# Blockwise-causal attention into a ReGLU layer on one core: two heads normalised in one piece, and new hand-listed orders for tiles 3 to 8

## The chip, the core and the metric

The kernel runs on one core of a Trainium2 chip. Its engines work side by side, each through its own instruction list, and wait for each other by semaphores: TensorE (PE) multiplies matrices into PSUM banks, VectorE (DVE), ScalarE (ACT) and GpSimd (POOL) work on elements, and SyncE (SP) issues transfers; ACT and POOL issue some as well. The metric is device microseconds of one execution, as the median of several runs.

## The reference

Eight batches of eight heads attend to themselves over 576 positions of 64 numbers, each block of 64 positions seeing its own and the earlier blocks. The heads are laid side by side to 4608 rows of 512, which go through a gated layer.

```python
scores = scale * np.matmul(q, k.transpose(0, 1, 3, 2))      # q, k, v: (8, 8, 576, 64)
mask = block_i >= block_j                                   # blocks of 64 positions
attn = np.exp(scores - max); attn = attn / (attn.sum(-1) + 1e-09)
x = np.matmul(attn, v).transpose(0, 2, 1, 3).reshape(4608, 512)
out = (np.maximum(x @ w_gate, 0.0) * (x @ w_val)) @ w_out   # 512 -> 1536 -> 512
```

## The kernel before

**Tiles.** The layer works on nine tiles of 512 rows: tiles 0 to 7 are the first 512 rows of each batch, and tile 8 is the 64 last rows of all eight batches together. While PE works on the layer of tile j, the attention of batch j + 1 (in the code `up`) is mixed into the same lists, and the loads and transposes of batch j + 2. From tile 3 on, pairs of output features are computed with seven products of half size in place of eight (`times`, `pair` and `seven_products`), so that DVE, ACT and POOL have adds and copies to do around them.

**Order.** Nothing decides the order at run time. Tiles 3 to 6 run one list of tokens, `ORDER_3_6`, tile 7 runs `ORDER_7` and tile 8 `ORDER_8`; `program(j)` turns each token into instructions, and each engine does its own in the listed order. The tokens that the text speaks of are these:

- `A2`: the scores of round 2 of a batch (a round is a pair of heads), L631, into two tiles of kind sc (two PSUM banks each) and two single banks; `E2t`, `E2u`, `E2f`, `E2s`: its exponentials on ACT (L636, L643); `C20`: zeros in a corner of the weights, a memset on DVE (L1516) or POOL (L1519).
- `V10`: head 0 of round 1 times v on PE (`head_av`, L779 and L793); a column of ones in v gives the sum of the weights as column 64. `N10`: that head is normalised on DVE (`normalise`: reciprocal L716, product into `xnat` L718, product of the last 64 rows into `xtail` L725).
- `T1`: `xnat` of round 1 is transposed into `xT` by a transfer on SP (L862); `T3` also transposes `xtail` (L765). `d0` and `d1` transpose q and k of the batch after (L519), `d2` and `d3` their tails (L524, L526); `l` and `w` load q, k and v by POOL's queue (L509).
- `g`, `v`, `r`, `h`: the plain products with the gate and value weights (L1339), relu, and their product (L1435). `X`, `Y`: sums of x that the seven products need (L1171), `U`: sums of weights (L979).
- `p54`: product 4 of pair 5 (L1363; each such token is two matmuls 128x256, and there are two of each). `p5a`, `p5u`, `p5w`: copies on ACT (L1385); `p5d`, `p5e`, `p5c`: adds on DVE (L1389); `p5r`: relu; `p5H`: product of the upper half with the relu (L1401, DVE or POOL); `p5L`: the lower half's relu and product in one DVE instruction (L1405).
- `s1002`: a part sum for the output products (quad 1, part 0, L1020, DVE or POOL). `M1`: two matmuls of output product 1 (L1061), six times `M1` making the product up; the third and sixth read pairs 4 and 5. `oa`, `ou`, `ow`, `oy`: copies on ACT (L1106; in tile 8 the last one in halves `oya` on ACT and `oyb` on DVE, L1118); `oc`, `od`, `oe`: adds on DVE (L1100), in tile 8 `oca` and `ocb` in halves. `S0`, `S1`, `S2`, `Sa`, `Sya` and so on: stores of the output (L906).

**Banks.** PSUM holds two sc tiles of two banks, one bank `one` and three banks `ffnp`. `AV_BANK` says into which kind `V` writes for each of the four rounds, `PAIR_BANK` and `OUT_BANK` the same for the seven products, and `SLOTS` which buffer each allocation of a kind takes. `ON_POOL` names the tokens that POOL does; the others of the kind are DVE's.

For round 1 the table gives each head an sc tile of its own, of which one bank is used, and `N10` and `N11` follow their heads separately. `normalise_two` and the branch `"sc2"` of `head_av` are in the code already, and no table uses them.

Of the kernel before, what the change touches and what calls it, by code (L numbers as in the profile page):

```python
# [17 lines left out]
def kernel(  # L18
# [24 lines left out]
    OBS = 5  # L43
    SLOTS = {
        "sc": (
            "010101010101010010101010101010101010101010101010101010101001100011000101"
            "1001100011000101100110001100010110011000110001011001011001000"
        ),
        "ffnp": (
            "021021021020210210210210210210120210120202010101210120201201120120210211"  # L50
            "201021102101020120120120121201202101202101202101210201201202120101212012"
            "021021020102121010210201201202120101212012021021020102121010210202102010"
            "2020201210"
        ),
        "ob": (
            "043210432104314021340123401321034120134021034013204103214013210341201340"
            "210340134013204230214302"
        ),
        "gate_sb": (
            "021021021021021021021021021021021021021201201210210212012012102102120120"  # L60
            "1201"
        ),
    }
# [23 lines left out]
        p17*2 p16*2 C00 C01 p1c k V00 N00 P v1*2 p1u p15*2 p1w p1d p14 V01 N01 p14 p1e
        p1L v1*2 r0 r1 p13*2 p1r v0*2 h1 A1 E1t v0*2 h0 p21*2 E1s p22*2 w1 p27*2 p2a
        p26*2 E1u l1 w2 p31 p1H l2 l3 p2c p31 g8 U05 l4 p2w p24*2 w3 s0002 p2u p2e p2L
        l5 l6 p25 g8 p25 p2d C11 p3a p36*2 p32 p37*2 E1f C10 V11 l7 N11 U06 l8 p3u p35  # L90
        p3w p35 p3d g8*2 r8 p23*2 p2H l9 p34*2 p3e p33*2 p3r p32 A2 E2t E2u p3c p3L v8*4
# [9 lines left out]
        p0u p05*2 p21 p0w p1u p21 p04*2 p0d p0e p2a p15*2 p1w p1d p22 p03 p22 p03 p0r
        p31 p14*2 p13*2 p1r p26 p31 p0L p27 p26 p27 p2c p1e p1H Y5 p1L p37*2 p0H s0002
        s0202 s0102 p32*2 p2u p25 p3a p3c p36 p25 p36 p2w p24*2 p2d p2e p51*2 p3w p3u
        p35*2 p3d p23*2 p2L p34*2 p5a p56 p33*2 p2r p2H p3e p3L p52 p57 p56 p41 p57 p41
# [7 lines left out]
        p04 p05*2 p0d p21 p1u p15*2 p31 p1w p1d p14*2 p1e p3a p04 p1L p0e p21 p2a p03*2
        p0r p0H p13 p02 p13 p1r p02 p0c P p1H p36 p26*2 p2u p27*2 p2w p41 p32 p25 p32
        p41 p4a p25 s0002 p0L s0102 p2d p3c p37*2 p3w p36 p3u p24*2 p2e p23*2 p2r p2H
        p34*2 p3e p35 p47 p35 p3d p22*2 p47 p2c p4w p3L p2L p42 p51*2 p5a p42 p33*2 p3r
        p3H p4c p46*2 p56 p44*2 p4u p4e p4L p56 p5u p57*2 p5w p45*2 p4d p55*2 p5d p54*2
# [38 lines left out]
        (6, 5): ('ffn', 'one', 'ffn'),
        (7, 0): ('ffn', 'one', 'one'),
        (7, 1): ('sc', 'sc', 'sc'),
        (7, 2): ('ffn', 'ffn', 'ffn'),
        (7, 3): ('one', 'ffn', 'sc'),
        (7, 4): ('ffn', 'one', 'ffn'),  # L160
        (7, 5): ('sc', 'sc', 'ffn'),
        (8, 0): ('one', 'sc', 'ffn'),
# [6 lines left out]
    ON_POOL = set(
        """  # L170
        33H 35H 3C00 3C01 3C10 3C11 3C20 3C21 3C30 3C31 3X4 3X6 3X7 3s0102
        3s0202 3s0302 3s1302 3s2202 3s2302 43H 45H 4C00 4C01 4C10 4C11 4C20 4C21
        4C30 4C31 4X4 4X6 4X7 4s0102 4s0202 4s0302 4s1302 4s2202 4s2302 53H 55H
        5C00 5C01 5C10 5C11 5C20 5C21 5C30 5C31 5X4 5X6 5X7 5s0102 5s0202 5s0302
        5s1302 5s2202 5s2302 63H 65H 6C00 6C01 6C10 6C11 6C20 6C21 6C30 6C31 6X4
        6X6 6X7 6s0102 6s0202 6s0302 6s1302 6s2202 6s2302 70H 72H 7X4 7X5 7X6
        7Y5 7Y7 7s0102 7s0202 7s0302 7s1002 7s1102 7s1202 7s1302 7s2302 80H 82H
        83H 8s0002 8s0102 8s1002 8s1202 U03 U06 U07 U46
        """.split()
    )  # L180
# [1636 lines left out]
```

## Time and profile before

| what | value |
|---|---|
| median of 3 runs | 344.85 us (344.63 to 344.87) |
| profiled execution, device time | 344.71 us |
| its span, first to last instruction | 342.8 us |
| granted TensorE clock, mean | 0.997 |

The profiled execution is one of its own, beside the three. The profile gives each engine's busy time in the span, the chain of work that ended last, the groups of instructions by line with their mean time, and, on request, the timeline of one engine: start, duration, engine, line, operation, what is written and read, and in brackets how long the engine had been idle and what it waited for. `x15` at the end of a timeline row means that fifteen instructions of one form in a row are shown as one. A queue name with q (`SPq`, `ACTq`) is an engine issuing transfers.

### The profile page before, as it was taken

The page shows a single profiled execution, that of the slowest core. Times are in us where ns is not written, and L with a number is a line of the kernel's source. Part 1 is how long each engine was busy: PE and PEld are TensorE (multiplying, and loading weights), DVE is VectorE, ACT ScalarE, POOL GpSimd, SP SyncE. Part 2 cuts the span into 40 slices and gives each one's busy share as a digit, 9 for nine tenths or more (in the row PEclk, how much of TensorE's full clock was granted, in tenths as well). Part 3 has the DMA queues.
Part 4 walks back from the last instruction along what each step waited for, and adds up shares of the span by engine and source line. Part 5 has one row for each costly group of instructions (what it writes and reads, how often), then busy time and mean ns, then how long its engine had stood idle before and what let it go on. Part 6 is the DMA issues. An engine that isn't in the chain of part 4 may idle for free.

```text
span 342.8 us, 8917 instructions
## 1 busy us (share of the span) xinstructions
PE 332.7 (97%) x3477; PEld 233.8 (68%) x3518; DVE 233.1 (68%) x540; ACT 210.8 (61%) x344; POOL 216.7 (63%) x272
## 2 busy tenths in 40 slices
PE   8899999999999999999999999999999999999994
PEld 4544455545545558777877787777777788888883
DVE  4854445668637887389538972898279958966992
ACT  4942757588325882778558764876488727637731
POOL 2766566488695912787778967986514694750631
PEclk9999999999999999999999999999999999999998
DMA  8999999999998999799899989996510140002004
GB/s 242 294 351 371 368 230 238 240 163 155 187 197 137 144 158 137 165 143 121 111 165 120 130 116 153 128 137 118 138 33 2 33 122 12 2 31 94 33 0 122
DMA packets 155337, 50.06 MB, mean 146 GB/s; under 512 B 134496, under 2 KB 151648, under 8 KB 155296
## 3 DMA queue, kind: packets, MB, share of 16 engines
q0 software_dynamic: 70576, 9.12, 43.6%
q1 hardware_dynamic: 77536, 32.52, 43.0%
q10 hardware_dynamic: 7184, 7.87, 7.8%
q8 instruction: 27, 0.44, 0.5%
q14 instruction: 14, 0.11, 0.1%
HBM read 37.75 MB, written 9.44 MB: 138 GB/s over the span
## 4 chain that ended last, share of the span: by engine, by line
PE 88%; issue 4%; DVE 2%; ACT 2%; POOL 2%; POOLq 0%; DVEq 0%; ACTq 0%
PE ffnp L1179 16%; PE ffnp L1363 9%; PE ffnp L1339 8%; PE sc L1363 8%; PE sc L1061 6%; PE ffnp L1282 6%; PE ffnp L1061 6%; PE one L1363 5%; PE one L1061 4%; PE sc L631 3%; PE one L631 2%; PE one L779 2%; PE ffnp L779 2%; PE one L1179 2%; PE sc L779 1%
## 5 line engine op out<-in xcount | busy, mean ns | idle before, releaser
L636 ACT ACTIVATE attnT<-sc 128x1024 bf16<-128x1024 f32 x56 | 56.7, 1036 | 0.0
L1189 ACT ACTIVATE gate_sb<-ffnp 128x512 bf16<-128x512 f32 x35 | 20.6, 599 | 27.3 <-PE ffnp L1179 24.4
L1179 PE MATMUL ffnp<-xT,wg 128*128 128x512 bf16 x130 | 36.2, 379 | 0.6
L1061 PEld LDWEIGHTS <-stage 128*128 128x128 bf16 x336 | 32.0, 98 | 4.1 <-issue 0.2
L1363 PEld LDWEIGHTS <-stage 128*128 128x128 bf16 x288 | 27.3, 98 | 7.8
L779 PEld LDWEIGHTS <-attnT 128*128 128x128 bf16 x640 | 26.3, 98 | 7.7 <-DVE xnat L718 1.2
L1179 PE MATMUL ffnp<-xT,wv 128*128 128x512 bf16 x108 | 31.3, 380 | 0.2
L1199 DVE TENSOR_TENSOR hT<-gate_sb,ffnp 128x512 bf16<-128x512 bf16 x28 | 19.2, 684 | 14.9 <-PE ffnp L1179 12.0
L1389 DVE TENSOR_TENSOR ob<-ffnp,ob 128x512 f32<-128x512 f32 x29 | 19.8, 684 | 12.6 <-ACT ob L1385 12.6
L509 POOL DMA_DIRECT2D v_bf<-in_v_dram x30 | 24.3, 829 | 6.0 <-PE sc L793 3.1
L1061 PEld LDWEIGHTS <-hT 128*128 128x128 bf16 x252 | 24.2, 98 | 5.3 <-DVE hT L1405 1.1
L1363 PEld LDWEIGHTS <-wg 128*128 128x128 bf16 x224 | 21.9, 98 | 5.1
L1363 PEld LDWEIGHTS <-wv 128*128 128x128 bf16 x224 | 21.5, 98 | 5.3 <-ACT attnT L636 1.1
L1106 ACT COPY ob<-sc 128x512 f32<-128x512 f32 x13 | 7.6, 586 | 28.4 <-PE sc L1061 27.0
L1519 POOL MEMSET attnT<- 64x256 bf16 x34 | 10.2, 314 | 23.4 <-ACT attnT L636 16.0
L1282 PE MATMUL ffnp<-wo,hT 128*128 128x512 bf16 x91 | 23.1, 379 | 0.2
L1179 PEld LDWEIGHTS <-wg 128*128 128x128 bf16 x144 | 13.3, 98 | 13.8 <-issue 0.5
L1179 PEld LDWEIGHTS <-wv 128*128 128x128 bf16 x144 | 13.0, 98 | 14.3 <-issue 1.5
L1334 ACT ACTIVATE gate_sb<-ffnp 128x512 bf16<-128x512 f32 x30 | 17.6, 603 | 8.1 <-PE ffnp L1363 4.6
L509 POOL DMA_DIRECT2D q_bf<-in_q_dram x20 | 18.0, 908 | 5.0 <-DVE recip L752 4.0
L643 ACT ACTIVATE attnT<-one 128x512 bf16<-128x512 f32 (+1 forms) x28 | 15.0, 537 | 9.8 <-PE ffnp L631 8.4
L1020 POOL TENSOR_TENSOR stage<-hT,stage 128x512 bf16<-128x512 bf16 x15 | 17.4, 1167 | 4.2 <-DVE stage L1020 3.6
(228 smaller groups left out, 918.3 us busy)
## 6 DMA issues: line engine op xcount, KB each, us to landing
out_dram<-ob ACTq DMA_DIRECT2D x28, 256.0 KB, 3.4
stage<-in_moe_w_val_dram SPq DMA_DIRECT2D x6, 512.0 KB, 8.7
stage<-in_moe_w_gate_dram SPq DMA_DIRECT2D x6, 512.0 KB, 8.2
stage<-in_moe_w_out_dram SPq DMA_DIRECT2D x6, 512.0 KB, 10.5
q_bf<-in_q_dram POOLq DMA_DIRECT2D x20, 128.0 KB, 4.7
k_bf<-in_k_dram POOLq DMA_DIRECT2D x20, 128.0 KB, 5.5
v_bf<-in_v_dram POOLq DMA_DIRECT2D x20, 128.0 KB, 5.7
stage<-in_v_dram SPq DMA_DIRECT2D x19, 128.0 KB, 5.6
```

The lines of the kernel that those rows point to most:

```text
L509: ins = nc.gpsimd.dma_start(dst, part_of)
L636: return lambda: nc.scalar.activation(at[:, :, lo : lo + 512], sc, AF.Exp, scale=scale)
L779: nc.tensor.matmul(av[:, p, :], at[:, col : col + 128], v_bf[b % 2][:, c, h, :], start=(p == 0), stop=(c == p), skip_group_check=True,)
L1061: nc.tensor.matmul(to, sums.of(c)[which][:, 128 * p : 128 * p + 128], right, start=first, stop=(c == 5), skip_group_check=True,)
L1179: nc.tensor.matmul(to, (wg, wv)[t][f // 4][:, c, 128 * (f % 4) : 128 * (f % 4) + 128], x[:, c], start=(c == 0), stop=(c == 3),)
L1189: nc.scalar.activation(gate_sb, gate, AF.Relu)
L1199: nc.vector.tensor_tensor(out=h, in0=gate_sb, in1=val, op=AX.mult)
L1282: nc.tensor.matmul(op, hT[f][:, 128 * s : 128 * (s + 1)], wo[f // 4][:, f % 4, n0:n1], start=(f == 0), stop=(f == 11),)
L1334: nc.scalar.activation(st[key], of, AF.Relu)
L1339: nc.tensor.matmul(to, (wg, wv)[t][f // 4][:, c, 128 * (f % 4) : 128 * (f % 4) + 128], x[:, c], start=(c == 0), stop=(c == 3),)
L1363: nc.tensor.matmul(st[key][:, 256 * k : 256 * k + 256], left[:, c, 128 * k : 128 * k + 128], right[:, c], start=new and (k, c) == (0, 0), ...
L1389: nc.vector.tensor_tensor(out=t, in0=st[n, of], in1=t, op=AX.add)
```

## The change

In tiles 3 to 6 the two heads of round 1 now write the two banks of one sc tile, one after the other, and one `N11` normalises both: a reciprocal of 128x10, a product of 128x512 into `xnat` and a product of 64x128 into `xtail`. `N10` is gone from the list, and `V10 V11 N11` stand together. Rounds 2 and 3 change the kinds of their banks. All three lists, the buffers in `SLOTS`, the kinds in `PAIR_BANK` and `OUT_BANK` and the placement on POOL or DVE are new:

- tiles 3 to 6: `C00`, `C10`, `C11`, `C20`, `X6` and `s0102` go from POOL to DVE, pair 1's H product and `s0002` from DVE to POOL;
- tile 7: `X7`, pair 3's H product and `s0002` to POOL; `Y5`, `Y7` and `s1202` to DVE;
- on SP the transposes were q, k, T1, T0, q and k tails, T2, T3, xtail; they are now q, T0, T1, k, q and k tails, T2, T3, xtail;
- the loads of q and k (`l`) stand earlier in a tile, those of v (`w`) later;
- tile 8: the store `Sa` moves from before the first `M5` to between `oya` and `Sya`, and `Sb` behind a further part of `M5`.

The matmuls are the same ones in another order.

```diff
     ORDER_3_6 = """
-        l0 A0 E0t E0u g0*2 p12 w0 p12 X5 X7 E0s E0f X6 X4 K g0*2 g1*2 p11*2 p1a g1*2
...
-        h8 p57 p51*2 p57 p52 E2s V10 N10 p5a p56*2 p5w d0 d1 T1 p5u s0202 p3H p52 p5c g9
-        p54*2 p5e l10 s1102 g9*3 p55*2 p5d C21 p5L s1002 E2f r9 s0302 s1202 A3 E3t v9
-        E3f U45 s0102 p53*2 p5r C20 v9 V21 v9 N21 v9 M1 h9 V20 M1*2 p5H s2102 s2002 E3s
...
+        A0 E0u g0*2 g1 g0 l0 l1 X5 X7 E0f g1*2 E0t E0s p12 p11 p12 p11 p1a l2 C01 l3 X6
...
+        v8*4 h8 p51 p57 p51 p3L p57 E2f E2s C20 V10 V11 N11 g9 p5a p56*2 p5w p54 p52 p54
+        g9*2 d0 g9 E2u C21 l10 p5u p5e T0 T1 p52 r9 p55*2 p5c A3 E3t p5d v9*2 p3H s1002
+        s1102 p5L p53*2 w4 w5 V21 U07 N21 U43 v9 M1 E3f p5r d1 d2 M1 v9 h9 s1202 M7 M1*2
...
     ORDER_7 = """
...
-        p47 p3r p3H p52 p5c p42*2 p5u p55 p4a p4c p46*2 p47 p55 p5w p54 p5d p54 p5e M1
-        s1002 s1202 s1102 p4w p4u p44*2 p4e p45 p53 p45 p4d p53 M1 p5r P p4L p5L p5H
-        M2*2 M7 p43 M7 p43 p4r p4H s2002 s2202 s2302 M1*4 oa M2*4 M6*6 s2102 M7*4 ou
...
+        p42 p4a p42 p4c p52 p57 p46 p5c p5u p55 p5w p55 p5d p46 s0202 p47*2 p54*2 p5e
+        p4u p4w p45*2 p4d M1 p44*2 p4e p3H p5L p4L M2 p53 M1 p43*2 p4r M7 p53 M2 p4H p2H
+        s1002 p5r P p5H M1*4 M2*3 s1102 M7 M2 s1202 s2002 s2202 oa M6*6 s2102 M7*4 ou
...
     ORDER_8 = """
...
-        p5e M2 p52 p43 p52 p5c p5L p53 p43 p4r p4H p53 p5r p5H M1*2 M2 M1*4 M2*4 s0202
-        s1002 s1202 oa s2002 s2202 M6*2 M7 s2102 M6*4 s1102 M7 s0302 s2302 M7*4 ou oca
-        Sa M5*5 ocb s1302 Sb ow M5 od M4 S2 M4*3 M3*3 oya Sya M4*2 oe S1 M3*3 oyb Syb
...
+        p33*2 p3r p3H s1002 p42 p4c p46*2 p56*2 p44*2 p4u p4e p57 p45 p57 p45 p4d p5u
+        p55*2 p5w p5d p52*2 p5c p54*2 p5e p43 p53 M2 p43 p53 p4L M1*2 M7 p5L p4r M2 p4H
+        p5r p5H M1*4 oa M2*2 s0202 s2002 s2202 oca M2 s1202 M2 M6*6 ou s1102 s2102 M7*5
+        M5 ow M5*3 ocb Sb s2302 s0302 s1302 M5*2 od S2 M4*4 M3*3 oya Sa Sya M4*2 oe S1
+        M3*3 oyb Syb
...
-    AV_BANK = {0: ('one', 'one'), 1: ('sc', 'sc'), 2: ('ffn', 'one'), 3: ('ffn', 'sc')}
+    AV_BANK = {0: ('one', 'one'), 1: ('sc2', 'sc2'), 2: ('sc', 'one'), 3: ('one', 'ffn')}
```

More of the change, by code (lines that the diff above doesn't have):

```diff
@@ L45 @@
         "sc": (
-            "010101010101010010101010101010101010101010101010101010101001100011000101"
-            "1001100011000101100110001100010110011000110001011001011001000"
+            "010101010101010010101010101010101010101010101010101010101010011101010101"
+            "101001110101010110100111010101011010011101010101100101001100"
         ),
@@ L50 @@
             "021021021020210210210210210210120210120202010101210120201201120120210211"
-            "201021102101020120120120121201202101202101202101210201201202120101212012"
-            "021021020102121010210201201202120101212012021021020102121010210202102010"
-            "2020201210"
+            "201021102101020120120120121201202101202101202101210221021202101210122012"
+            "201202120102010221022102120210121012201220120212010201022102011200201210"
+            "012120"
         ),
@@ L56 @@
             "043210432104314021340123401321034120134021034013204103214013210341201340"
-            "210340134013204230214302"
+            "210340130413042034021340"
         ),
         "gate_sb": (
-            "021021021021021021021021021021021021021201201210210212012012102102120120"
+            "021021021021021021021021021021021021021210210202102101021021210210210120"
             "1201"
@@ L85 @@
     ORDER_3_6 = """
-        l0 A0 E0t E0u g0*2 p12 w0 p12 X5 X7 E0s E0f X6 X4 K g0*2 g1*2 p11*2 p1a g1*2
[L87 to L91, printed above, removed]
@@ L92 @@
-        h8 p57 p51*2 p57 p52 E2s V10 N10 p5a p56*2 p5w d0 d1 T1 p5u s0202 p3H p52 p5c g9
-        p54*2 p5e l10 s1102 g9*3 p55*2 p5d C21 p5L s1002 E2f r9 s0302 s1202 A3 E3t v9
-        E3f U45 s0102 p53*2 p5r C20 v9 V21 v9 N21 v9 M1 h9 V20 M1*2 p5H s2102 s2002 E3s
-        C30 N20 U47 M1*3 M7*2 T0 d2 d3 E3u C31 V30 M7 V31 N30 T2 oa N31 s2202 s2302 M6*6
-        ou M7*3 ow M2 M5*5 M4 M5 M4*3 od S2 M4*2 oe S1 M2 U46 U43 M3 U07 w4 s1302 M3*5
-        M2*4 oc oy S0 w5 T3 U03
+        A0 E0u g0*2 g1 g0 l0 l1 X5 X7 E0f g1*2 E0t E0s p12 p11 p12 p11 p1a l2 C01 l3 X6
@@ new lines @@
+        X4 C00 K k g0 g1 p1c l4 l5 p17*2 p16*2 V00 N00 w0 v1*2 P p1u p15*2 v1 p1w U05
+        U06 p1d V01 N01 l6 l7 r0 r1 p14*2 p1e p1L v1 p13*2 p1r h1 p1H v0*2 A1 E1t v0*2
+        p21*2 E1s h0 U45 p22*2 p27*2 p2a p26*2 p2c p31*2 p2w p24*2 g8*2 p2u p25 p3a E1u
+        p2e p2L p36*2 p3u p25 p2d p37*2 g8 p3w p35*2 p3d g8 r8 p23*2 p2H p34 E1f p34 p3e
+        p33*2 p3r p32 U03 l8 w1 w2 C11 p32 p3c U46 l9 s0102 C10 w3 s0002 s0202 A2 E2t
+        v8*4 h8 p51 p57 p51 p3L p57 E2f E2s C20 V10 V11 N11 g9 p5a p56*2 p5w p54 p52 p54
@@ L98 @@
+        g9*2 d0 g9 E2u C21 l10 p5u p5e T0 T1 p52 r9 p55*2 p5c A3 E3t p5d v9*2 p3H s1002
+        s1102 p5L p53*2 w4 w5 V21 U07 N21 U43 v9 M1 E3f p5r d1 d2 M1 v9 h9 s1202 M7 M1*2
+        p5H s2002 s2102 E3s C30 M7 d3 V20 N20 T2 M2 M1*2 E3u C31 V30 N30 V31 oa N31 M7
+        M6*2 s2202 M6*4 M7*2 ou M2 M7 M5*4 ow M4 M5*2 U47 od M4*5 oe s0302 s1302 S2 M3*2
+        s2302 M3*2 S1 M3*2 M2 T3 M2*3 oc oy S0
     """
     ORDER_7 = """
-        p11 X5 X7 X6 X4 p01*2 p0a p02*2 p11 p1a p0c p12*2 p1c p06*2 p16*2 p07*2 p17*2
@@ L101 @@
[L101 to L104, printed above, removed]
-        p47 p3r p3H p52 p5c p42*2 p5u p55 p4a p4c p46*2 p47 p55 p5w p54 p5d p54 p5e M1
-        s1002 s1202 s1102 p4w p4u p44*2 p4e p45 p53 p45 p4d p53 M1 p5r P p4L p5L p5H
@@ L107 @@
-        M2*2 M7 p43 M7 p43 p4r p4H s2002 s2202 s2302 M1*4 oa M2*4 M6*6 s2102 M7*4 ou
-        M5*3 ow M5*3 od S2 oc M4*6 s1302 s0302 oe M3*4 S1 Y7 Y6 M3*2 oy S0
+        X5 X7 p02 p07 X6 p01*2 Y5 X4 p0a p02 p0c p12 p11*2 p12 p1a p1c p06*2 p07 p17*2
+        p16*2 p0u p05*2 p0w p0d p21 p04*2 p0e p1u p15*2 p1w p1d p21 p2a p14*2 p1e p1L
+        p03 p22 p03 p0r p0H p22 p2c p13*2 p37 p1r p1H s0002 p31*2 p26 p32 p26 p37 p0L
+        s0102 p32 p3a p3c p27 p36 p27 p2u p3w p2w p25 p36 p3u p25 p2d p34*2 p24*2 p2e
@@ L109 @@
+        p41 p35*2 p3d p51 p23 p51 p5a p57 p23 p2r p33*2 p3r p56*2 p41 p3e p2L p3L p52
+        p42 p4a p42 p4c p52 p57 p46 p5c p5u p55 p5w p55 p5d p46 s0202 p47*2 p54*2 p5e
+        p4u p4w p45*2 p4d M1 p44*2 p4e p3H p5L p4L M2 p53 M1 p43*2 p4r M7 p53 M2 p4H p2H
+        s1002 p5r P p5H M1*4 M2*3 s1102 M7 M2 s1202 s2002 s2202 oa M6*6 s2102 M7*4 ou
+        M5*5 ow M5 od S2 M4*5 s2302 s1302 s0302 M3 M4 M3 oe S1 Y7 M3*4 oy S0 Y6 oc
     """
     ORDER_8 = """
-        p01 p31 p01 p0a p17 p11*2 p1a X4 p07 p17 p07 p0w p06 p12 p06 p0u p12 p1c p16*2
@@ L112 @@
[L112 to L116, printed above, removed]
-        p5e M2 p52 p43 p52 p5c p5L p53 p43 p4r p4H p53 p5r p5H M1*2 M2 M1*4 M2*4 s0202
@@ L118 @@
-        s1002 s1202 oa s2002 s2202 M6*2 M7 s2102 M6*4 s1102 M7 s0302 s2302 M7*4 ou oca
-        Sa M5*5 ocb s1302 Sb ow M5 od M4 S2 M4*3 M3*3 oya Sya M4*2 oe S1 M3*3 oyb Syb
+        p01 X4 p01 p11 p0a p17*2 p1w p07 p12 p07 p11 p1a p06 p31 p06 p12 p1c p31 p16*2
+        p0u p05*2 p0w p0d p14 p04*2 p1u p15 p0e p15 p14 p1d p1e p1L p21 p3a p03 p02 p03
+        p21 p0r p36 p13*2 p02 p37 p27 p2a p26*2 p0c p0H p1r p36 p32 p27 p37 p1H s0002
+        p0L s0102 p2u p25*2 p32 p2w p2d p24*2 p41 p3c p3w p34 p2e p23 p34 p3u p3e p35
@@ L120 @@
+        p23 p51 p2r P p2H p35 p3d p41 p4a p51 p47 p22*2 p5a p2c p3L p2L p47 p4w p42
+        p33*2 p3r p3H s1002 p42 p4c p46*2 p56*2 p44*2 p4u p4e p57 p45 p57 p45 p4d p5u
[3 more added lines that the diff above has]
+        M3*3 oyb Syb
     """
@@ L142 @@
         (3, 3): ('ffn', 'sc', 'ffn'),
-        (3, 5): ('ffn', 'one', 'ffn'),
+        (3, 5): ('ffn', 'one', 'sc'),
         (4, 1): ('sc', 'sc', 'ffn'),
@@ L146 @@
         (4, 3): ('ffn', 'sc', 'ffn'),
-        (4, 5): ('ffn', 'one', 'ffn'),
+        (4, 5): ('ffn', 'one', 'sc'),
         (5, 1): ('sc', 'sc', 'ffn'),
@@ L150 @@
         (5, 3): ('ffn', 'sc', 'ffn'),
-        (5, 5): ('ffn', 'one', 'ffn'),
+        (5, 5): ('ffn', 'one', 'sc'),
         (6, 1): ('sc', 'sc', 'ffn'),
@@ L154 @@
         (6, 3): ('ffn', 'sc', 'ffn'),
[L155 to L162, printed above, removed]
+        (6, 5): ('ffn', 'one', 'sc'),
+        (7, 0): ('ffn', 'one', 'ffn'),
+        (7, 1): ('sc', 'sc', 'ffn'),
+        (7, 2): ('ffn', 'one', 'one'),
+        (7, 3): ('sc', 'ffn', 'ffn'),
+        (7, 4): ('ffn', 'ffn', 'ffn'),
+        (7, 5): ('sc', 'one', 'ffn'),
+        (8, 0): ('one', 'sc', 'sc'),
         (8, 1): ('ffn', 'ffn', 'sc'),
@@ L165 @@
         (8, 3): ('ffn', 'ffn', 'ffn'),
-        (8, 4): ('sc', 'ffn', 'one'),
-        (8, 5): ('ffn', 'ffn', 'sc'),
+        (8, 4): ('sc', 'one', 'ffn'),
+        (8, 5): ('ffn', 'sc', 'ffn'),
     }
@@ L170 @@
         """
[L171 to L178, printed above, removed]
+        31H 33H 35H 3C01 3C21 3C30 3C31 3X4 3X7 3s0002 3s0202 3s0302 3s1302
+        3s2202 3s2302 41H 43H 45H 4C01 4C21 4C30 4C31 4X4 4X7 4s0002 4s0202
+        4s0302 4s1302 4s2202 4s2302 51H 53H 55H 5C01 5C21 5C30 5C31 5X4 5X7
+        5s0002 5s0202 5s0302 5s1302 5s2202 5s2302 61H 63H 65H 6C01 6C21 6C30
+        6C31 6X4 6X7 6s0002 6s0202 6s0302 6s1302 6s2202 6s2302 70H 72H 73H 7X4
+        7X5 7X6 7X7 7s0002 7s0102 7s0202 7s0302 7s1002 7s1102 7s1302 7s2302 80H
+        82H 83H 8s0002 8s0102 8s1002 8s1202 U05 U06 U43 U46 U47
         """.split()
     )
-    OUT_BANK = {(2, 'v'): 'ffn', (2, 'w'): 'ffn', (2, 'x'): 'one', (3, 'v'): 'one', (3, 'w'): 'sc', (3, 'x'): 'ffn', (4, 'v'): 'one', (4, 'w'): 'sc', (4, 'x'): 'ffn', (5, 'v'): 'one', (5, 'w'): 'sc', (5, 'x'): 'ffn', (6, 'v'): 'one', (6, 'w'): 'sc', (6, 'x'): 'ffn', (7, 'v'): 'one', (7, 'w'): 'ffn', (7, 'x'): 'ffn', (8, 'v'): 'sc', (8, 'w'): 'ffn', (8, 'x'): 'one'}
+    OUT_BANK = {(2, 'v'): 'ffn', (2, 'w'): 'ffn', (2, 'x'): 'one', (3, 'v'): 'ffn', (3, 'w'): 'sc', (3, 'x'): 'ffn', (4, 'v'): 'ffn', (4, 'w'): 'sc', (4, 'x'): 'ffn', (5, 'v'): 'ffn', (5, 'w'): 'sc', (5, 'x'): 'ffn', (6, 'v'): 'ffn', (6, 'w'): 'sc', (6, 'x'): 'ffn', (7, 'v'): 'one', (7, 'w'): 'sc', (7, 'x'): 'ffn', (8, 'v'): 'ffn', (8, 'w'): 'one', (8, 'x'): 'one'}
     UP_MEM = {
```

## The prediction

> **What bounds the kernel now.** I read the page's busy times and chain first, then the stretches of tiles 4, 7 and 8 side by side, then TensorE's (PE's) timeline for gaps, and last the queues that release it.
>
> ```profile
> span 342.8 us, 8917 instructions
> PE 332.7 (97%) x3477; PEld 233.8 (68%) x3518; DVE 233.1 (68%) x540; ACT 210.8 (61%) x344; POOL 216.7 (63%) x272
> PE 88%; issue 4%; DVE 2%; ACT 2%; POOL 2%; POOLq 0%; DVEq 0%; ACTq 0%
> ```
>
> PE is busy for 97% of the span and is 88% of the chain that ended last; the other engines have a third of their time free. The next view gives, for a stretch, its length and each engine's busy time (instructions), then granted clock, DMA share and GB/s. The first row is tile 4 with the attention of batch 5, the second tile 7, the third tile 8 and the end.
>
> ```profile
> 174.71:210.32 35.61, 35.35 (x412) 27.43 (x416) 24.95 (x56) 24.56 (x40) 28.59 (x36) 1.00 1.30 130
> 281.56:309.70 28.14, 27.91 (x256) 24.63 (x255) 22.92 (x39) 15.18 (x28) 16.07 (x14) 1.00 0.09 31
> 309.70:342.80 33.10, 28.10 (x252) 24.15 (x249) 22.42 (x41) 15.95 (x29) 10.13 (x9) 0.97 0.20 56
> ```
>
> Tile 4 leaves PE 0.26 us of 35.61; tiles 7 and 8 leave more. To find waits I use the pitch, not the durations, because a matmul's row is longer than the time until the next one starts:
>
> ```profile
> 204.32 0.82 PE L1061 MATMUL one<-wo,stage 128*128 128x256 bf16 x6
> 204.97 0.38 PE L1061 MATMUL ffnp<-wo,hT 128*128 128x256 bf16 x2
> ```
>
> Six matmuls take 204.97 - 204.32 = 0.65 us, so 0.109 us each; two last 0.38, so the end of one lies 0.38 - 0.109 = 0.27 after its start. A row that starts later than 0.109 us per matmul after the one before holds a wait. The pairs below are where that happens at the end.
>
> ```profile
> 301.13 0.27 PE L1061 MATMUL ffnp<-wo,hT 128*128 128x256 bf16 x1
> 301.64 1.81 PE L1061 MATMUL ffnp<-wo,hT 128*128 128x256 bf16 x15 [0.23 <-DVE hT L1405]
> ...
> 325.82 0.38 PE L1363 MATMUL ffnp<-perm,stage 128*128 128x256 bf16 x2
> 326.18 0.60 PE L1363 MATMUL ffnp<-perm,wv 128*128 128x256 bf16 x4
> ...
> 328.14 0.93 PE L1061 MATMUL ffnp<-wo,hT 128*128 128x256 bf16 x7
> 329.38 1.81 PE L1061 MATMUL ffnp<-wo,hT 128*128 128x256 bf16 x15 [0.31 <-DVE hT L1405]
> ...
> 333.80 1.36 PE L1061 MATMUL ffnp<-stage 128*128 128x256 bf16 x11
> 335.51 1.03 PE L1061 MATMUL sc<-stage,hT 128*128 128x256 bf16 x8 [0.35 <-ACT ob L1106]
> ...
> 337.03 0.60 PE L1061 MATMUL sc<-stage,hT 128*128 128x256 bf16 x4
> 337.66 0.82 PE L1061 MATMUL ffnp<-wo,stage 128*128 128x256 bf16 x6
> ```
>
> Tile 7: 301.64 - 301.13 - 0.11 = 0.40. Tile 8: 326.18 - 325.82 - 0.22 = 0.14; 329.38 - 328.14 - 0.76 = 0.48; 335.51 - 333.80 - 1.20 = 0.51; 337.66 - 337.03 - 0.44 = 0.19. Together 1.72 us: with the same matmuls, that is about all that any order of tiles 7 and 8 can win.
>
> **Normalising two heads at once.** In tiles 3 to 6 round 1's six DVE instructions become three, on twice the elements.
>
> ```profile
> L716 DVE RECIPROCAL recip<-sc 128x5 f32<-128x5 f32 x14 | 2.7, 192 | 2.6 <-PE sc L793 2.3
> L718 DVE TENSOR_TENSOR xnat<-sc,recip 128x256 bf16<-128x256 f32 x18 | 7.6, 424 | 0.6
> L725 DVE TENSOR_TENSOR xtail<-sc,recip 64x64 bf16<-64x64 f32 x14 | 2.9, 204 | 0.0
> L1389 DVE TENSOR_TENSOR ob<-sc,ob 128x512 f32<-128x512 f32 x21 | 14.4, 684 | 5.7 <-PE sc L1363 5.1
> ```
>
> Now 2 x (192 + 424 + 204) = 1640 ns. The trace has none of the new forms. Each lies between one of its old halves and two of them; for the product, an operation on 512 elements per partition out of the same bank (684) is a nearer lower end than 424. So the three take between 192 + 684 + 204 = 1080 and 1640 ns; I take 1250, a little above the lower end since twice the elements cost 684 instead of 2 x 424. DVE gains about 0.4 us a tile (0 to 0.56). DVE has 35.61 - 24.95 = 10.7 us free in tile 4, and nothing on PE waits there: worth 0 on the path. Cover gone, the bound is 4 x 0.56 = 2.2 us, which PE's 0.26 us per tile does not have to give. The sc tile is held until one product is done, so its slot comes free later than the first head's did; scores and plain products that need a slot stand many matmuls behind in the list.
>
> **The new order of tiles 3 to 6.** PE gets the same 412 matmuls a tile. POOL gives up memsets, a sum of x and one part sum to DVE and takes a product: DVE 24.95 us plus a few tenths still fits under 35.61. On SP the transposes of x for heads T0 and T1 now stand ahead of the k transpose, and all of T2, T3 and the tails behind it.
>
> ```profile
> 194.77 3.12 SPq L519 DMA_TRANSPOSE kTm<-k_bf  x1
> ...
> 203.20 3.02 SPq L862 DMA_TRANSPOSE xT<-xnat  x2
> ...
> 211.09 0.39 PE L1339 MATMUL ffnp<-xT,wg 128*128 128x512 bf16 x1
> ...
> xT<-xnat SPq DMA_TRANSPOSE x2, 4.2
> ```
>
> The queue carries the same transposes. The last of the two at 203.20 is issued near 205.0 and, by the last row (median us from issue to landing in that stretch), lands near 209.2; PE asks for it at 211.09 or later: 1.9 us in hand. The queue's work from the first x transpose to the tails stays the same sum, so I take 0, between -0.1 (what small waits a tile has) and the whole k block arriving late, 3.12 - 1.9 = 1.2 us per tile boundary. The loads of q and k go to POOL's queue at the tile's start instead of spread over it, v's later; what is behind them on POOL (memsets, part sums) serves products several microseconds later.
>
> **Tile 7.** PE's third M1 pair needs DVE's two-input products p5L and p4L.
>
> ```profile
> 299.70 0.68 DVE L1389 TENSOR_TENSOR q_bf<-ffnp,q_bf 128x512 f32<-128x512 f32 x1
> 300.30 1.28 DVE L1405 SCALAR_TENSOR_TENSOR hT<-ob,k_bf 128x512 bf16<-128x512 f32 x2
> 301.50 1.28 DVE L1401 TENSOR_TENSOR hT<-gate_sb,q_bf 128x512 bf16<-128x512 bf16 x2
> ...
> 299.06 1.16 POOL L1020 TENSOR_TENSOR stage<-hT 128x512 bf16<-128x512 bf16 x1
> ```
>
> DVE's pitch is 0.60 (300.30 - 299.70, 1.28 for two) with 0.69 for the last. In the new order DVE does, after the last matmul of p54: p5e, p4d, p4e, p5L, p4L. From that matmul's start: 0.27 end plus 0.04 to the engine, 3 x 0.60, 0.60, 0.69, 0.05 back to PE = 3.45 us. PE does 26 matmuls in between and arrives after 27 x 0.109 = 2.94: a wait of 0.51, against 0.40 now: +0.1.
>
> **Tile 8.** Here the list after the last matmul of p45 gives DVE p4d, p5d, p5c, p5e, p4L, p5L: 0.31 + 4 x 0.60 + 0.60 + 0.69 + 0.05 = 4.05, against 32 x 0.109 = 3.49 on PE: 0.56 (0.48 now). M6 then wants the part sum s2202 behind p4H, p5H, s0202 and s2002:
>
> ```profile
> 329.24 1.29 DVE L1401 TENSOR_TENSOR hT<-gate_sb,q_bf 128x512 bf16<-128x512 bf16 x2
> 330.44 0.41 DVE L1020 TENSOR_TENSOR stage<-stage,hT 128x512 bf16<-128x512 bf16 x1
> 330.78 0.42 DVE L1020 TENSOR_TENSOR stage<-hT 128x512 bf16<-128x512 bf16 x1
> 331.23 0.42 DVE L1020 TENSOR_TENSOR stage<-stage,hT 128x512 bf16<-128x512 bf16 x1
> ...
> 333.36 1.47 ACTq L906 DMA_DIRECT2D out_dram<-ob  x2
> 334.87 0.59 ACT L1106 COPY ob<-sc 128x512 f32<-128x512 f32 x1 [1.49 <-DVE stage L1020]
> ```
>
> From p4H's start the same five took 331.23 + 0.42 - 329.24 = 2.41 us; p4H starts 0.14 before PE goes on, and PE has 19 matmuls (2.07) until it needs the sum: 0.25 more. The 0.51 goes: the copy at 334.87 that released PE stood behind two output stores (Sa, Sb) issued by ACT at 333.36, 1.47 us long; Sa moves behind the copy of the last block and Sb behind the one that PE waits for. The last block's 0.19 stays, and the second half of od (0.27 + 0.04 + 0.69 + 0.05 against 9 x 0.109) costs 0.07. Sum 0.56 + 0.25 + 0.07 + 0.19 = 1.07 against 0.14 + 0.48 + 0.51 + 0.19 = 1.32: -0.25. Sa's two stores now go out beside the last ones: 1.47 / 2 = 0.73 us on each of two queues, which wait for copies anyway; from 0 to +0.2, I take 0.05.
>
> **Sum.** 0 (tiles 3 to 6) + 0.1 - 0.25 + 0.05 = -0.1 us, against 344.71 us of the profiled execution, whose span is 342.8 with 1.9 around it. The median shown, 344.85, is 0.14 above that execution: 344.7 us.
>
> **A rule against it.** Two rows of tile 3, DVE and POOL, meet:
>
> ```profile
> 156.79 1.34 DVE L1405 SCALAR_TENSOR_TENSOR hT<-ob,ob 128x512 bf16<-128x512 f32 x1
> ...
> 156.42 1.17 POOL L1401 TENSOR_TENSOR hT<-gate_sb,ob 128x512 bf16<-128x512 bf16 x1
> ```
>
> The DVE product takes 1.34 us instead of 1.28 - 0.60 = 0.68: it began while POOL's ran to 157.59. The Trainium skill, GPSIMD Engine Reference, section Specifications, says that GpSimd shares its SBUF interfaces with VectorE and contends with DVE instructions that have two SBUF inputs; the trace agrees (+0.66 us). By it, any product moved under a POOL operation would pay this.
>
> **Rivals.** (A, slower) POOL's sums run into p5L or p4L. Now POOL's last sum of tile 7 ends at 300.22, 0.08 us before the products at 300.30, and tile 8 is similar:
>
> ```profile
> 328.63 0.69 DVE L1405 SCALAR_TENSOR_TENSOR hT<-ob,k_bf 128x512 bf16<-128x512 f32 x1
> ...
> 327.30 1.15 POOL L1020 TENSOR_TENSOR stage<-stage,hT 128x512 bf16<-128x512 bf16 x1
> ```
>
> In the new order a chain of two products and two sums (4 x 1.16) ends on POOL about when DVE comes to p5L in tile 7; 0.2 us later and p5L pays up to 0.66 in front of a PE that waits already. Against it: DVE's own chain would have to be that much ahead. In tile 8 0.45 us are in hand. Both hit: +0.5 and +0.6, so 345.8 us. (B, slower) The k and x transposes arrive late at three boundaries: 3 x 1.2 = 3.6, so 348.3. For it: the order on SP changes; against it: its sum doesn't. (C, faster) The new lists keep DVE ahead in tiles 7 and 8, and only the 0.19 at the end remains: -1.5, so 343.2. Against it: the chains of 3.45 and 4.05 above. (D) The change doesn't do what it says: the joint product takes 2 x 424 or more, and nothing is saved on DVE. The time is as forecast, since 10.7 us cover it.
>
> **Chances.** Forecast 0.60, D 0.06, A 0.22, B 0.04, C 0.08. Under 0.2% (0.7 us) a measurement of this kernel hardly differs from no change. Faster 0.10 (C and 0.02 of the forecast), slower 0.28 (A's larger part 0.20, B, and 0.04 of the forecast), same 0.62. The forecast's own range is 344.2 to 345.2. The range 343.9 to 346.2 takes in A with 0.4 us beside it and half of what C promises, and leaves out B and most of C.
>
> **What would show it.** Right: tile 4 again 35.5 to 35.7 us; one product of about 700 ns (650 to 850) in place of two of 424; a wait before the M1 pair of 0.5 in tile 7 and 0.6 in tile 8; no wait of 0.5 behind an output copy. Wrong: an L1405 of over 1 us in tile 7 or 8 with POOL beside it (A), the first plain product of a tile waiting for xT (B), or a PE timeline of tile 8 with no waits but the last (C).

## The result and the profile after

The changed kernel takes 345.75 us (median of 20 runs, 345.10 to 346.77), the kernel before 344.75 us (20 runs): ratio 1.0028, 95% interval 1.0019 to 1.0036. It is slower by about 1.0 us, where no change was forecast. The profiled execution took 345.86 us, against 344.71 before. Ratios and intervals, here and below, leave out the few runs that took over 1.5% longer than the fastest of their kernel, and they are not quotients of the printed medians.

The page of the changed kernel gives PE still nearly all of the span, and its tiles one by one (length, then busy time and instructions of PE, PE's loads, DVE, ACT, POOL, then clock, DMA share, GB/s) show where the time went. The rows are tiles 3, 4, 5, 6, 7, and 8 with the end.

```profile
span 344.1 us, 8941 instructions
PE 335.6 (98%) x3518; PEld 234.0 (68%) x3518; DVE 234.5 (68%) x543; ACT 210.0 (61%) x344; POOL 214.4 (62%) x257
```

```profile
139.21:175.16 35.95, 35.86 (x417) 27.40 (x416) 24.77 (x56) 24.99 (x41) 28.49 (x34) 1.00 1.16 133
175.16:210.97 35.81, 35.76 (x417) 27.51 (x417) 25.31 (x57) 24.47 (x40) 27.56 (x32) 1.00 1.37 131
210.97:247.00 36.03, 35.75 (x417) 27.47 (x416) 25.30 (x57) 24.43 (x40) 24.92 (x29) 1.00 1.20 135
247.00:282.51 35.51, 35.51 (x418) 27.59 (x418) 25.45 (x60) 24.42 (x40) 21.75 (x22) 1.00 0.17 47
282.51:310.67 28.16, 27.70 (x255) 24.54 (x253) 22.40 (x36) 14.97 (x27) 14.99 (x13) 1.00 0.10 34
310.67:344.10 33.43, 28.48 (x254) 24.34 (x251) 23.81 (x44) 15.57 (x29) 10.12 (x9) 0.99 0.19 57
```

Between their first scores tiles 3, 4 and 5 took 35.70, 35.61 and 35.62 us before; they are 0.25, 0.20 and 0.41 us longer now. Tile 6 runs the same list, with the sums `U` added, and is no longer than before (35.5). What it lacks is the loads of a later batch: DMA share 0.17 in place of 1.16 to 1.37. PE's timeline of tile 5, and behind the dots the same place of tile 6, shows the wait:

```profile
225.20 0.38 PE L1339 MATMUL ffnp<-xT,wg 128*128 128x512 bf16 x1
225.86 0.60 PE L1363 MATMUL one<-xT,stage 128*128 128x256 bf16 x4 [0.28 <-DVE ob L1389]
...
261.23 0.38 PE L1339 MATMUL ffnp<-xT,wg 128*128 128x512 bf16 x1
261.45 0.60 PE L1363 MATMUL one<-xT,stage 128*128 128x256 bf16 x4
```

A 128x512 matmul holds PE for 261.45 - 261.23 = 0.22 us; in tile 5 the next one, p23, starts 0.44 us later than that. In tiles 3 and 4 the same gap is 0.25 and 0.21: 0.9 us together. p23 adds to the bank that p2d has to read first, and p2d is an add on DVE (L1389). DVE's timeline of the same two places, p2e, p2L and p2d in this order:

```profile
223.06 0.69 DVE L1389 TENSOR_TENSOR ob<-sc,ob 128x512 f32<-128x512 f32 x1 [0.94 <-PE sc L1363]
223.85 1.35 DVE L1405 SCALAR_TENSOR_TENSOR hT<-ob,ob 128x512 bf16<-128x512 f32 x1
225.12 0.68 DVE L1389 TENSOR_TENSOR ob<-one,ob 128x512 f32<-128x512 f32 x1
...
259.09 0.69 DVE L1389 TENSOR_TENSOR ob<-sc,ob 128x512 f32<-128x512 f32 x1 [0.94 <-PE sc L1363]
259.88 0.69 DVE L1405 SCALAR_TENSOR_TENSOR hT<-ob,ob 128x512 bf16<-128x512 f32 x1
260.50 0.68 DVE L1389 TENSOR_TENSOR ob<-one,ob 128x512 f32<-128x512 f32 x1
```

p2L took 1.35 us in place of 0.69 (1.23 and 1.12 in tiles 3 and 4), and p2d starts late for that. POOL was issuing loads beside it, and no arithmetic:

```profile
222.27 0.95 POOL L509 DMA_DIRECT2D k_bf<-in_k_dram  x1
223.21 1.76 POOL L509 DMA_DIRECT2D v_bf<-in_v_dram  x2
224.95 0.66 POOL L509 DMA_DIRECT2D k_bt<-in_k_dram  x1
```

Tile 7's wait is 302.58 - 301.73 - 0.22 = 0.63 us, against 0.40. The reason is on DVE and POOL: the sum s1102 began on POOL at 300.21 and ended at 301.37, and p5L, begun at 301.12, took 0.80 us (1.40 for the two in place of 1.28).

```profile
301.73 0.38 PE L1061 MATMUL ffnp<-wo,hT 128*128 128x256 bf16 x2
302.58 1.05 PE L1061 MATMUL sc<-wo,hT 128*128 128x256 bf16 x8 [0.46 <-DVE hT L1405]
...
301.12 1.40 DVE L1405 SCALAR_TENSOR_TENSOR hT<-ob,k_bf 128x512 bf16<-128x512 f32 x2
...
299.10 2.27 POOL L1020 TENSOR_TENSOR stage<-hT 128x512 bf16<-128x512 bf16 x2
```

Tile 8, PE's timeline:

```profile
328.16 0.38 PE L1363 MATMUL sc<-xTt,attnT 128*128 128x256 bf16 x2
328.46 0.38 PE L1363 MATMUL ffnp<-xTt,stage 128*128 128x256 bf16 x2
...
329.99 0.38 PE L1061 MATMUL ffnp<-wo,hT 128*128 128x256 bf16 x2
330.26 0.28 PE L1061 MATMUL one<-wo,hT 128*128 128x256 bf16 x1
330.86 0.94 PE L1061 MATMUL one<-wo,hT 128*128 128x256 bf16 x7 [0.32 <-DVE hT L1405]
...
332.51 1.73 PE L1061 MATMUL one<-stage 128*128 128x256 bf16 x12
...
336.48 1.04 PE L1061 MATMUL ffnp<-stage,hT 128*128 128x256 bf16 x8
337.49 0.81 PE L1061 MATMUL one<-wo,stage 128*128 128x256 bf16 x6
338.14 0.60 PE L1061 MATMUL ffnp<-stage,hT 128*128 128x256 bf16 x4
338.77 0.81 PE L1061 MATMUL one<-wo,stage 128*128 128x256 bf16 x6
```

The waits are 0.08, 0.05 and 0.49 (p4L and p5L: 0.54), 0.25 inside the group of twelve at 332.51 (1.73 against 11 x 0.109 + 0.28), 0.14 and 0.19: 1.20 against 1.32 before. The wait of 0.51 for a copy behind two stores is gone, as worked out. In sum: 0.9 + 0.23 - 0.12 = 1.0 us, about what the medians show. The two profiled spans lie 1.24 us apart: 0.21 ahead of tile 3, where both run the same lists, 0.85 in tiles 3 to 5, nothing in tile 6, 0.17 in tile 7, -0.11 in tile 8's products and 0.13 behind the last of them. (The rows of tiles 7 and 8 in the prediction begin 0.10 and 0.25 us behind the first products of these tiles, at 281.46 and 309.45, so the lengths of tiles 7 and 8 can't be compared row by row.)

The joint piece itself, in tile 5 of the changed kernel (first three rows), and the first and last of the six instructions of the two heads apart at the same place (kernel "heads apart" below):

```profile
231.32 0.22 DVE L819 RECIPROCAL recip<-sc 128x10 f32<-128x10 f32 x1 [0.25 <-PE sc L793]
231.57 0.69 DVE L820 TENSOR_TENSOR xnat<-sc,recip 128x512 bf16<-128x512 f32 x1
232.18 0.27 DVE L826 TENSOR_TENSOR xtail<-sc,recip 64x128 bf16<-64x128 f32 x1
```

```profile
231.14 0.20 DVE L716 RECIPROCAL recip<-sc 128x5 f32<-128x5 f32 x1
...
232.39 0.20 DVE L725 TENSOR_TENSOR xtail<-sc,recip 64x64 bf16<-64x64 f32 x1
```

Joint: 0.22 + 0.69 + 0.27 = 1.18 us of instructions, from 231.32 to 232.45. Apart: from 231.14 to 232.59. DVE gains 1.45 - 1.13 = 0.32 us a tile.

### The profile page after: what moved, and what is told of

Read it like the earlier page. It is cut to its first block, busy times and chain, and to the rows that moved or that the text cites. A ratio compares the mean times of both kernels' runs of the same rounds, so it can differ in the third digit from the quotient of the medians.

```text
span 344.1 us, 8941 instructions
## 1 busy us (share of the span) xinstructions
PE 335.6 (98%) x3518; PEld 234.0 (68%) x3518; DVE 234.5 (68%) x543; ACT 210.0 (61%) x344; POOL 214.4 (62%) x257
## 4 chain that ended last, share of the span: by engine, by line
PE 87%; issue 4%; DVE 4%; ACT 2%; POOL 1%; POOLq 0%; DVEq 0%
PE ffnp L1179 16%; PE ffnp L1363 9%; PE sc L1363 8%; PE ffnp L1339 8%; PE sc L1061 8%; PE ffnp L1061 7%; PE ffnp L1282 6%; PE one L1363 5%; PE sc L631 4%; PE one L779 2%; PE one L631 2%; ACT attnT L595 2%; PE one L1179 2%; PE ffnp L779 1%; PE sc L779 1%
## 5 line engine op out<-in xcount | busy, mean ns | idle before, releaser
L1179 PE MATMUL ffnp<-xT,wg 128*128 128x512 bf16 x140 | 37.8, 379 | 0.0
L1061 PEld LDWEIGHTS <-stage 128*128 128x128 bf16 x336 | 32.3, 98 | 4.9 <-DVE stage L1020 0.4
L1363 PEld LDWEIGHTS <-stage 128*128 128x128 bf16 x288 | 28.1, 98 | 8.7 <-issue 1.3
L1179 PE MATMUL ffnp<-xT,wv 128*128 128x512 bf16 x112 | 32.0, 380 | 0.0
L1519 POOL MEMSET attnT<- 64x256 bf16 x18 | 5.2, 306 | 39.0 <-ACT attnT L636 23.4
L1106 ACT COPY ob<-sc 128x512 f32<-128x512 f32 x15 | 8.8, 586 | 32.4 <-PE sc L1061 32.4
L1389 DVE TENSOR_TENSOR ob<-ffnp,ob 128x512 f32<-128x512 f32 x28 | 19.1, 687 | 3.3 <-ACT ob L1385 2.1
L1389 DVE TENSOR_TENSOR ob<-sc,ob 128x512 f32<-128x512 f32 x23 | 15.8, 686 | 6.8 <-PE sc L1363 4.1
```

What stands on the lines that cost most here:

```text
L1061: nc.tensor.matmul(to, sums.of(c)[which][:, 128 * p : 128 * p + 128], right, start=first, stop=(c == 5), skip_group_check=True,)
L1179: nc.tensor.matmul(to, (wg, wv)[t][f // 4][:, c, 128 * (f % 4) : 128 * (f % 4) + 128], x[:, c], start=(c == 0), stop=(c == 3),)
L1363: nc.tensor.matmul(st[key][:, 256 * k : 256 * k + 256], left[:, c, 128 * k : 128 * k + 128], right[:, c], start=new and (k, c) == (0, 0), ...
L1389: nc.vector.tensor_tensor(out=t, in0=st[n, of], in1=t, op=AX.add)
```

## The experiments

The theory was: the loads that POOL issues beside p2L draw it out, and through p2d PE waits. The rivals were the orders of tiles 7 and 8, the joint piece, and a p23 that stands too close behind p2d in any case. The kernel before was timed beside each group.

**Middle alone** (tiles 3 to 6 changed, tiles 7 and 8 as before):

```diff
-    ORDER_7, ORDER_8 and the banks, buffers and places of tiles 7 and 8: changed kernel
+    ORDER_7, ORDER_8 and the banks, buffers and places of tiles 7 and 8: kernel before
```

> Tiles 3 to 6 of the changed kernel, with tiles 7 and 8 of the kernel before. Theory: the loss lies in tiles 3 to 5, where PE waited 0.25 + 0.21 + 0.44 = 0.9 us for p2d. Then this kernel is 0.5 to 1.2 us slower than before, the three waits are there, and tile 6 has none. Rival: the loss lies in the new orders of tiles 7 and 8 (their stores, or POOL beside p5L): then it is within 0.2 us of the kernel before.

345.75 us against 344.95, ratio 1.0022 (1.0003 to 1.0040). In its trace tiles 3 and 4 wait 0.25 and 0.21 us, but tile 5 doesn't: there p2L took 0.69 with the loads at the same distance as in the changed kernel (issues 0.64 us ahead of it and 0.23 us into it; 0.64 and 0.23 there).

```profile
223.59 0.69 DVE L1405 SCALAR_TENSOR_TENSOR hT<-ob,ob 128x512 bf16<-128x512 f32 x1
...
222.95 1.77 POOL L509 DMA_DIRECT2D v_bf<-in_v_dram  x2
```

So most of the loss lies in the middle, by the times. This one trace shows less: tiles 3 to 5 are 0.41 us longer than before, and 0.56 us more than before lie behind PE's last product. The same meeting does not always cost the same. The spread of the runs says nothing on that: it is 1.67 us for the changed kernel and 1.55 for the kernel before (20 runs each).

**All loads held** until p2d is done:

```diff
-                    after(ins, behind)
+                    after(ins, behind or (HOLD.pop() if HOLD else None))   # HOLD: the add p2d
```

> The changed kernel, with the loads that POOL issues at that place (l8, w1, w2, l9, w3) held back until p2d is done; nothing else is moved. Theory: POOL's issuing of loads draws p2L (L1405 with two SBUF inputs) out from 0.69 to 1.12 to 1.35 us, and p2d and PE's p23 come late for that. Then p2L takes 0.69 in tiles 3 to 5, the three waits (0.9 us together) go, and the time is 0.6 to 1.0 us under that of the changed kernel, about equal to before (-0.2 to +0.3 us). Rival 1: p23 stands too close behind p2d in the new order whatever POOL does: the waits stay at 0.2 or more. Rival 2: the loads come late instead, and a k transpose or the products with v wait: then over 1 us slower than before.

346.11 us, ratio 1.0027 (1.0002 to 1.0052): no gain. The three waits at p23 are gone and p2L takes 0.69 in tiles 3 to 5, which speaks against rival 1. (The traced execution is a long one, 348.95 us; it has lost 3.1 us by the start of tile 3, and only what comes after is read here.) But the sums s0002 and s0202, behind the loads on POOL, ran later, onto p5L. DVE's timeline of tile 4, then POOL's, then PE's:

```profile
197.10 1.70 DVE L1405 SCALAR_TENSOR_TENSOR hT<-ob,ob 128x512 bf16<-128x512 f32 x1
...
197.04 1.20 POOL L1020 TENSOR_TENSOR stage<-hT 128x512 bf16<-128x512 bf16 x1
...
200.25 0.60 PE L1363 MATMUL ffnp<-perm,stage 128*128 128x256 bf16 x4
200.86 0.27 PE L631 MATMUL one<-qTm,kTm 64*128 64x256 bf16 x1
```

p5L takes 1.70 us, and the scores of round 3 wait for the adds behind it: 200.86 is 0.17 us later than four matmuls after 200.25, where the changed kernel has 0.10, and from there to the next plain product PE takes 0.93 us instead of 0.77. Between their first scores tiles 3, 4 and 5 take 36.25, 35.83 and 35.85 us. The wait had moved; this was not among the expectations.

**One load held** (w2 alone, until p2L is done):

```diff
-                    after(ins, behind)
+                    after(ins, HOLD.pop() if HOLD and (t, c) == (2, 2) else behind)   # HOLD: p2L
```

> The changed kernel, with one load of v alone (w2) held back until p2L is done, about 0.5 us later than before; the sums s0002 and s0202 behind it move by no more than that and end ahead of p5L. Theory: p2L takes 0.69 in tiles 3 to 5, p2d and PE's p23 are in time, no new wait appears, and tiles 3 to 5 take 35.6 us each: 0.6 to 1.0 us faster than the changed kernel, so within 0.3 us of the kernel before. Rival: the sums, moved by 0.5 us, meet p5L as they did where all loads were held (1.39 to 1.74 us there) and PE waits at the scores of round 3 by 0.2 to 0.5 us a tile: no gain.

344.93 us against 345.01: ratio 1.0000 (0.9991 to 1.0010). Tiles 3 to 5 of its trace, then tile 5's p2L and POOL's loads:

```profile
139.93:175.64 35.71, 35.71 (x418) 27.43 (x418) 24.22 (x55) 24.91 (x41) 29.34 (x34) 1.00 1.45 132
175.64:211.24 35.60, 35.60 (x419) 27.52 (x418) 24.60 (x57) 24.42 (x40) 27.63 (x32) 1.00 1.53 131
211.24:246.83 35.59, 35.59 (x417) 27.48 (x417) 24.61 (x57) 24.42 (x40) 25.00 (x29) 1.00 1.24 139
```

```profile
224.12 0.69 DVE L1405 SCALAR_TENSOR_TENSOR hT<-ob,ob 128x512 bf16<-128x512 f32 x1
...
223.50 0.89 POOL L509 DMA_DIRECT2D v_bf<-in_v_dram  x1
225.10 0.88 POOL L509 DMA_DIRECT2D v_bf<-in_v_dram  x1 [0.72 <-DVE hT L1405]
```

Holding one load for 0.72 us gives back the whole loss, and the tiles are as long as in the kernel before. The load ahead of it, begun 0.62 us before p2L and still going, did no harm. So the loss comes from the issue of the load that begins in p2L. In all three kernels with w2 held (this one and two below) p2L takes 0.69 in tiles 3 to 5, nine times out of nine.

**Which load.** With l8 behind w1 and w2, the issue that begins in p2L is one of k:

```diff
-        l8 w1 w2 C11
+        w1 w2 l8 C11
```

> The changed kernel, with POOL's load of k (l8) behind the two of v (w1, w2), so that the issue that begins about 0.2 us into p2L is one of k and not the second of v. Theory A: any load that POOL begins to issue inside p2L draws it out: p2L stays at 1.1 to 1.35 us in tiles 3 to 5, the waits at p23 stay, and the time is that of the changed kernel. Theory B: only the v loads do (their target rows have gaps): p2L takes 0.69, the waits go, 0.6 to 0.9 us faster than the changed kernel.

345.80 us, ratio 1.0031 (1.0016 to 1.0047). p2L takes 1.25, 1.13 and 1.30 us in tiles 3 to 5: theory A; it isn't the target of the load.

**When.** With l9 ahead of w1 the issue begins with p2L:

```diff
-        l8 w1 w2 C11 p32 p3c U46 l9
+        l8 l9 w1 w2 C11 p32 p3c U46
```

> The changed kernel with POOL's short load l9 ahead of w1 and w2, so that a load begins within 0.1 us of the start of p2L and the next one only 0.88 us later, when p2L should be over. So far issues that began 0.23 to 0.37 us into the product drew it out to 1.1 to 1.35 us; one that began 0.39 to 0.54 us in, or 0.3 us and more ahead of it, did not (0.69). Theory A: what matters is an issue that begins in the first 0.37 us: p2L takes 1.0 us or more here as well, the waits at p23 stay. Theory B: the damage is done some 0.2 us after an issue begins, and only if the product has not yet read most of its input: p2L is again drawn out, by 0.2 to 0.4 us. Theory C: a product and an issue that begin together do not meet: p2L 0.69, no wait at p23, and the time is that of before within 0.3 us.

345.73 us, ratio 1.0020 (1.0000 to 1.0041). p2L takes 1.24, 1.11 and 1.11 us, with issues that began 0.11 us into it, and 0.01 and 0.02 ahead of it; PE waits 0.26, 0.21 and 0.21 us. Theory A again.

**Heads apart**, with the collision and then without it:

```diff
-        V10 V11 N11          AV_BANK 1: ('sc2', 'sc2')
+        V10 N10 V11 N11      AV_BANK 1: ('sc', 'sc')
```

> The changed kernel, with round 1's two heads normalised one after the other again, each in an sc tile of its own (V10 N10 V11 N11). Theory: the joint normalisation saves DVE 0.3 to 0.5 us a tile, but nothing on PE waits there, so the time is that of the changed kernel within 0.3 us and the waits at p23 in tiles 3 to 5 stay. Rival: the joint piece holds the sc tile or DVE longer and costs the time: then this one is 0.7 us faster or more.

346.18 us, ratio 1.0031 (1.0012 to 1.0050), like the changed kernel: the joint piece isn't the loss. In its trace tiles 3 and 4 wait at p23 as before, and tile 5 doesn't (p2L 0.69). Here PE waited behind the heads, for the row product at the first one's end (L725), 0.11, 0.11, 0.32 and 0.10 us in tiles 3 to 6, which the joint piece spares it.

> The changed kernel with w2 held until p2L is done, and round 1's heads normalised one after the other (V10 N10 V11 N11, an sc tile each). It prices the joint piece alone, with POOL's collision out of the way. Theory: the three instructions on both heads save DVE 0.3 to 0.5 us a tile; in this order PE needs an sc tile for pair 5's last product just behind, where the kernel with heads apart and the collision waited 0.10 to 0.32 us for the last row product (L725). Then this one shows that wait in each of tiles 3 to 6, no wait at p23, and is 0.3 to 0.8 us slower than the kernel with w2 held. Rival: the wait came from the collision upstream; without it PE finds the tile free and the two kernels are within 0.2 us.

344.96 us against 344.84, ratio 1.0008 (0.9979 to 1.0037): the rival holds. With w2 held that wait is left in tile 6 alone, at 0.10 us:

```profile
266.30 0.38 PE L1363 MATMUL one<-perm,wv 128*128 128x256 bf16 x2
266.62 0.39 PE L1363 MATMUL sc<-xT,wg 128*128 128x256 bf16 x2
```

So the joint piece alone is worth about 0.1 us in the whole kernel, by the traces; the times can't show so little.

**The stores of tile 8 alone**, on the kernel before:

```diff
-        ou oca Sa M5*5 ocb s1302 Sb ow M5 od
+        ou oca M5*5 ocb s1302 ow Sa Sb M5 od
```

> The kernel before, with the stores Sa and Sb of tile 8 moved behind the copy ow; nothing else. Theory: PE's wait of 0.51 us at the copy (L1106) goes, since the copy no longer stands behind two stores on ACT: 0.3 to 0.55 us faster than before. Rival: what PE waits for next (the add od, or the last copies behind the moved stores) takes it back: within 0.15 us of before.

> The kernel before with the stores Sa and Sb behind the copy ow once more, because the interval of its first timing (0.9965 to 1.0006) leaves open whether it beats before. Theory: 0.3 to 0.5 us faster than before, as the trace of the first one has it (PE's last matmul 0.38 us nearer to the start of tile 3). Rival: the last stores, now with two more beside them, land later and take it back: within 0.15 us of before.

344.53 us against 344.95 (ratio 0.9985, 0.9965 to 1.0006), and 344.51 against 344.84 (0.9992, 0.9970 to 1.0014). Both medians are 0.3 to 0.4 us lower and both intervals hold 1: likely a gain, not shown by the times. In both traces PE takes 28.65 us from tile 8's first product to the end of its last one, against 29.02 before, and what follows is no longer. In the trace of the second timing the wait of 0.51 us is gone; 335.00 follows 333.69 by the 12 matmuls alone, and 0.14 us appear behind the next group:

```profile
333.69 1.47 PE L1061 MATMUL ffnp<-stage 128*128 128x256 bf16 x12
335.00 1.04 PE L1061 MATMUL sc<-stage,hT 128*128 128x256 bf16 x8
336.02 0.81 PE L1061 MATMUL ffnp<-wo,stage 128*128 128x256 bf16 x6
```

**Both repairs together** (tiles 3 to 6 changed with w2 held, tiles 7 and 8 as before with those stores moved):

> Tiles 3 to 6 of the changed kernel with w2 held until p2L is done, and tiles 7 and 8 of the kernel before with the stores Sa and Sb behind the copy ow. Theory: the middle is even with before and the stores give 0.4 to 0.5 us: 0.2 to 0.6 us faster than before, the same as the kernel before with those stores moved. Rival: the middle keeps a loss of 0.3 us or more, and this one is no faster than before.

345.00 us against 345.01, ratio 0.9999 (0.9988 to 1.0009): a miss. Its waits on PE are those of the stores kernel, yet the times don't show it. In its one trace 4.65 us pass behind PE's last product, against 4.37 before; whether that takes the gain back in the other runs is open. No version here beats the kernel before beyond its interval.

## Why the prediction was wrong

- **The step that failed** is in "The new order of tiles 3 to 6", on the loads: they were priced at nothing because "what is behind them on POOL (memsets, part sums) serves products several microseconds later". That looks at what waits behind the loads in POOL's queue. The price was beside them, on another engine: 0.9 us in tiles 3 to 5 through p2L, p2d and p23. The term was 0 with an upper end for the k block on SP; none of that was for POOL's issues. The prediction also had the loads of q and k "at the tile's start"; the trace has l8, w1, w2, l9 and w3 back to back from 11.3 to 15.5 us into tile 5 (222.27 to 226.49), across p2L. The sign named for being right, tile 4 at 35.5 to 35.7 us, failed by that: it took 35.81.
- **The rule against it** was weighed with rows where POOL computes, and carried into tiles 7 and 8 only. The rule in the Trainium skill, GPSIMD Engine Reference, section Specifications, names VectorE instructions with two SBUF inputs, and p2L is one. The Trainium skill, SBUF — State Buffer, section Who interferes with whom, has such an instruction contend with a GpSimd instruction that reads SBUF and not with one that only writes it; of making descriptors, which is what it has GpSimd do for a load, it says, as an inference, that this needs the write interface. By that, an issue of loads should have left p2L alone. The runs disagree for p2L: 1.11 to 1.35 us beside an issue, 0.69 with the one load held.
- **Rival A** had the right kind of event at the wrong place and with other partners. Its place in tile 7 did come, at the small end: p5L 0.80 us instead of 0.69, wait 0.63 instead of the worked-out 0.51. In tile 8 it did not come. That 345.8 us was its price is a coincidence of sums.
- **Tile 8** came out by its terms: 0.56 for p4L and p5L (measured 0.54), 0.25 for s2202 (0.25), 0.51 gone, 0.19 at the end (0.19). The add od cost 0.14, twice its term, and 0.08 came from an add ahead of a bank (L1389) that had no term. -0.12 in place of -0.25. The 0.05 for the moved stores is not settled: 4.50 us pass behind PE's last product, against 4.37 before, and the other traces with the old end of the list or the new one have 4.39 to 4.93.
- **The joint piece:** 1.18 us against 1.25 forecast, inside its bounds; 0.32 us of DVE saved against 0.4; off the path, as said, but for 0.1 us in tile 6. Rival D did not come.
- **B** did not come: with one load held the tiles take 35.6 us, so the transposes on SP cost nothing. **C** did not either: the waits in tiles 7 and 8 stand. With the load held the ratio is 1.0000, the forecast for all the rest of the change.

## What to carry to other kernels

When work moves in a queue, look at what runs beside its new place on the engine that it shares something with, and not only at what stands behind it. Where PE takes a bank again soon after an add on DVE, look at the fp32 products with two SBUF inputs ahead of that add on DVE and keep POOL's work, the issuing of loads included, from meeting them; here, holding one load for 0.7 us was enough. Holding more than that one moved the collision on. A product that is drawn out costs nothing by itself: the kernel before has one of 1.33 to 1.34 us in each of tiles 3 to 6 (the prediction's row at 156.79 is the first), and they are as long as with w2 held.
